# Rebuilding the first part of a fused attention-and-MLP kernel: projections during the layernorm, a software-pipelined MLP and gate, operands of the first head pair staged ahead

## The chip, the cores and the metric

The kernel runs on one core of one Trainium2 chip. The metric is device time in microseconds (us): the median over the executions of one kernel, beside the kernel before on the same chip. Executions are sorted into a fast and a slow state; for this one-core kernel, slow means over 1.5% above the fastest execution of the same kernel. All executions that verdicts use are of the fast state. A profile is one execution of its kernel, with one exception (named below) a fast one; three kernels ran only once, so their state is unknown. Engines are PE (TensorE matmuls), PEld (its weight loads), DVE (VectorE), ACT (ScalarE), POOL (GpSimd) and SP (SyncE); "SPq" and "ACTq" are the queues in which SyncE and ScalarE issue DMAs. PEclk or "clock" is the TensorE clock granted, as a share of full speed.

## The reference

Forward and backward pass of one block, sequence 2048, width 512, 32 heads of 16, MLP width 1792, all in bf16. The kernel returns the output and the gradients of x, wqkv, wo, w1, b1, w2 and b2.

```
xn  = layernorm(x)
qkv = xn @ wqkv                                # attention branch
s   = softmax(q k^T / 4) v @ wo
y   = layernorm(xn)                            # gate branch
g   = silu(gelu(y @ w1 + b1) @ w2 + b2)
out = x + s * g                                # and the vjp of all this for grad_out
```

The first part, which the change rebuilds, makes xn, y, q, k and v, the MLP's hidden layer, the gate, and d = (grad_out * g) @ wo^T. Attention (16 pairs of heads, forward and backward together) follows and takes most of the time; the weight gradients close the kernel. Attention reads its operands from scratch tensors in HBM, which the first part fills.

## The kernel before

Each part of the first stage runs over all 2048 rows (16 tiles of 128) before the next starts. Cuts are marked.

```python
def ln_batch(src_of_t, dst, rstd_all, tagn):
    for t in range(NT):
        nc.vector.bn_stats(...);  nc.vector.bn_aggr(...)
    nc.scalar.activation(out=rstd_all[:], in_=mv[:, :, 1], func=ACT.Sqrt, ...)
    nc.vector.reciprocal(out=rstd_all[:], in_=rstd_all[:])
    for t in range(NT):
        nc.vector.tensor_scalar(out=dst[:, t, :], in0=src_of_t(t), scalar1=mv[:, t, 0:1],
                                scalar2=rstd_all[:, t:t + 1], op0=ALU.subtract, op1=ALU.mult)
ln_batch(..., xn, ...)
for t in range(NT): transpose_to(nc, psT, xnT, xn[:, t, :], ...)    # TensorE transposes
ln_batch(..., y, ...)
for t in range(NT): transpose_to(nc, psT, yT, y[:, t, :], ...)
# ... k and v of 16 tiles, then a maximum of |k|^2 over all rows, then q of 16 tiles (needs it) ...
for sh in range(2):                                   # halves of 1024 rows
    for fc in range(FC):                              # w1: 14 blocks
        h1row = wk.tile([128, S // 2], bf16, name="h1row")     # 3 buffers
        # 2 x (4 matmuls, + b1 on VectorE, gelu on ScalarE), store to H1T_s
    for t8 in range(8):                               # w2, 14 matmuls, then the gate in one chain
        # m_bf = ps + b2; sg = sigmoid(m_bf); gB0 = m_bf * sg; dso = dot * gB0
        # transpose dso; q1 = ((1 - sg) * gB0 + sg); gB1 = q1 * dot; store
        # projection of the tile before
# attention then loads pair 0 from HBM, lays it out in Pad and transposes it by DMA, all 2048 rows
```

Of the kernel before, what the change touches and what calls it, by code (L numbers as in the profile page):

```python
# [16 lines left out]
NT = S // 128  # L17
# [19 lines left out]
def ln_tile(nc, wk, x_t, out_t, rstd_col, eps_t):  # L37
    st = wk.tile([128, nc.vector.BN_STATS_DIM], f32, name="ln_st")
    mv = wk.tile([128, nc.vector.BN_AGGR_DIM], f32, name="ln_mv")
    nc.vector.bn_stats(out=st[:], in_=x_t)  # L40
    nc.vector.bn_aggr(out=mv[:], in_=st[:])
    nc.scalar.activation(out=rstd_col, in_=mv[:, 1:2], func=ACT.Sqrt, bias=eps_t[:], scale=1.0)
    nc.vector.reciprocal(out=rstd_col, in_=rstd_col)
    nmr = wk.tile([128, 1], f32, name="ln_nmr")
    nc.vector.scalar_tensor_tensor(out=nmr[:], in0=mv[:, 0:1], scalar=-1.0, in1=rstd_col, op0=ALU.mult, op1=ALU.mult)
    nc.scalar.activation(out=out_t, in_=x_t, func=ACT.Identity, bias=nmr[:], scale=rstd_col)


def transpose_to(nc, psp, dst3, src_nat, ident, nblk, t, eng_toggle):
    pt = psp.tile([128, nblk, 128], bf16, name="tp_ps", tag="tp")  # L50
    for b in range(nblk):
        nc.tensor.transpose(pt[:, b, :], src_nat[:, b * 128:(b + 1) * 128], ident[:])
    if eng_toggle % 2 == 0:
        nc.vector.tensor_copy(out=dst3[:, :, t * 128:(t + 1) * 128], in_=pt[:])
    else:
        nc.scalar.copy(out=dst3[:, :, t * 128:(t + 1) * 128], in_=pt[:])


def phase_pre(ctx, tc, k, A_x, A_wqkv, A_wo, B_w1, B_b1, B_w2, B_b2, grad_out, dbg):
    nc = tc.nc  # L60
    x2 = A_x.flatten_outer_dims()
    go2 = grad_out.flatten_outer_dims()
    with ExitStack() as c1:
        pA = c1.enter_context(tc.tile_pool(name="preA", bufs=1))
        xnT = pA.tile([128, IC, S], bf16, name="xnT")
        dsoT = pA.tile([128, IC, S], bf16, name="dsoT")
        yT = pA.tile([128, IC, S], bf16, name="yT")
        psT = c1.enter_context(tc.tile_pool(name="pre_psT", bufs=2, space=PSUM))
        psA = c1.enter_context(tc.tile_pool(name="pre_psA", bufs=5, space=PSUM))
        wts = c1.enter_context(tc.tile_pool(name="pre_w", bufs=1))  # L70
        wqkv_sb = wts.tile([128, IC, 3 * D], bf16, name="wqkv_sb")
        w1_sb = wts.tile([128, IC, F], bf16, name="w1_sb")
        w2_sb = wts.tile([128, FC, D], bf16, name="w2_sb")
        wo_sb = wts.tile([128, IC, D], bf16, name="wo_sb")
        mlp_big = c1.enter_context(tc.tile_pool(name="mlp_big", bufs=1))
        mlp_wk = c1.enter_context(tc.tile_pool(name="mlp_wk", bufs=3))

        with ExitStack() as c0:
            big0 = c0.enter_context(tc.tile_pool(name="pre_ln", bufs=1))
            wk0 = c0.enter_context(tc.tile_pool(name="pre_lnwk", bufs=4))  # L80
            xin = c0.enter_context(tc.tile_pool(name="pre_xin", bufs=4))
            xv = x2.rearrange("(t p) d -> p t d", p=128)
            xq = []
            for q4 in range(4):
                xt4 = xin.tile([128, 4, D], bf16, name="xt4")
                (nc.sync if q4 % 2 == 0 else nc.scalar).dma_start(out=xt4[:], in_=xv[:, q4 * 4:(q4 + 1) * 4, :])
                xq.append(xt4)
                if q4 == 0:
                    nc.scalar.dma_start(out=wqkv_sb[:], in_=A_wqkv.rearrange("(c p) f -> p c f", p=128))
            nc.scalar.dma_start(out=w1_sb[:], in_=B_w1.rearrange("(c p) f -> p c f", p=128))  # L90
            nc.sync.dma_start(out=w2_sb[:], in_=B_w2.rearrange("(c p) d -> p c d", p=128))
            nc.scalar.dma_start(out=wo_sb[:], in_=A_wo.rearrange("(c p) b -> p c b", p=128))
            xn = big0.tile([128, NT, D], bf16, name="xn")
            y = big0.tile([128, NT, D], bf16, name="y")

            def ln_batch(src_of_t, dst, rstd_all, tagn):
                st = big0.tile([128, NT, nc.vector.BN_STATS_DIM], f32, name="ln_st" + tagn)
                mv = big0.tile([128, NT, nc.vector.BN_AGGR_DIM], f32, name="ln_mv" + tagn)
                for t in range(NT):
                    nc.vector.bn_stats(out=st[:, t, :], in_=src_of_t(t))  # L100
                    nc.vector.bn_aggr(out=mv[:, t, :], in_=st[:, t, :])
                nc.scalar.activation(out=rstd_all[:], in_=mv[:, :, 1], func=ACT.Sqrt, bias=k.eps_t[:], scale=1.0)
                nc.vector.reciprocal(out=rstd_all[:], in_=rstd_all[:])
                for t in range(NT):
                    nc.vector.tensor_scalar(out=dst[:, t, :], in0=src_of_t(t), scalar1=mv[:, t, 0:1], scalar2=rstd_all[:, t:t + 1],
                                            op0=ALU.subtract, op1=ALU.mult)
            ln_batch(lambda t: xq[t // 4][:, t % 4, :], xn, k.rstd1, "1")
            for t in range(NT):
                transpose_to(nc, psT, xnT, xn[:, t, :], k.ident_bf, IC, t, 1)
            ln_batch(lambda t: xn[:, t, :], y, k.rstd2, "2")  # L110
            for t in range(NT):
                transpose_to(nc, psT, yT, y[:, t, :], k.ident_bf, IC, t, 1)
            nc.sync.dma_start(out=k.XN_s.rearrange("(t p) d -> p t d", p=128), in_=xn[:])
            nc.scalar.dma_start(out=k.Y_s.rearrange("(t p) d -> p t d", p=128), in_=y[:])

        with ExitStack() as c0:
            big = c0.enter_context(tc.tile_pool(name="p15_big", bufs=1))
            wk = c0.enter_context(tc.tile_pool(name="p15_wk", bufs=3))
            stg = c0.enter_context(tc.tile_pool(name="p15_stg", bufs=1))
            nc.vector.tensor_scalar(out=wqkv_sb[:, :, 0:D], in0=wqkv_sb[:, :, 0:D], scalar1=0.25, scalar2=None, op0=ALU.mult)  # L120
            NS = [stg.tile([128, NPAIR, 4, 2, NATW], bf16, name=f"NS{i}") for i in range(2)]
            for i in range(2):
                nc.gpsimd.memset(NS[i][:, :, :, :, 0:1], 1.0)
            NQ = [stg.tile([128, NPAIR, 4, 2, 17], bf16, name=f"NQ{i}") for i in range(2)]
            kmaxrun = big.tile([128, H], f32, name="kmaxrun")
            nc.vector.memset(kmaxrun[:], 0.0)
            for t in range(NT):
                pk = psA.tile([128, 512], f32, name="pk", tag="mm")
                pv = psA.tile([128, 512], f32, name="pv", tag="mm")
                for ic in range(IC):  # L130
                    nc.tensor.matmul(pk[:], lhsT=xnT[:, ic, t * 128:(t + 1) * 128], rhs=wqkv_sb[:, ic, D:2 * D],
                                     start=(ic == 0), stop=(ic == IC - 1))
                for ic in range(IC):
                    nc.tensor.matmul(pv[:], lhsT=xnT[:, ic, t * 128:(t + 1) * 128], rhs=wqkv_sb[:, ic, 2 * D:3 * D],
                                     start=(ic == 0), stop=(ic == IC - 1))
                ns = NS[(t // 4) % 2]
                kpv = ns[:, :, t % 4, :, :]
                nc.scalar.copy(out=kpv[:, :, :, 1:17], in_=pk[:].rearrange("p (a j c) -> p a j c", a=NPAIR, j=2))
                nc.vector.tensor_copy(out=kpv[:, :, :, 17:33], in_=pv[:].rearrange("p (a j c) -> p a j c", a=NPAIR, j=2))
                if t % 4 == 3:  # L140
                    (nc.sync if (t // 4) % 2 == 0 else nc.scalar).dma_start(
                        out=k.NAT_s[:, :, t - 3:t + 1, :].rearrange("a p t c -> p a t c"), in_=ns[:].rearrange("p a t j c -> p a t (j c)"))
                sq = wk.tile([128, H, DH], f32, name="sqk")
                kk = kpv[:, :, :, 1:17]
                nc.gpsimd.tensor_tensor(out=sq[:].rearrange("p (a j) c -> p a j c", j=2), in0=kk, in1=kk, op=ALU.mult)
                kn2 = wk.tile([128, H], f32, name="kn2")
                nc.vector.reduce_sum(out=kn2[:], in_=sq[:], axis=AX.X)
                nc.vector.tensor_tensor(out=kmaxrun[:], in0=kmaxrun[:], in1=kn2[:], op=ALU.max)
# [25 lines left out]
        with ExitStack() as c0:  # L174
# [29 lines left out]
            for sh in range(2):  # L204
# [15 lines left out]
                for t8 in range(8):  # L220
# [23 lines left out]
                    if t >= 1:  # L244
                        do_proj(t - 1)
# [316 lines left out]
def attention_core(ctx, tc, NAT_s, NATQ_s, Oall, dQall, dKVT_out, ident_f32, H1T_s, GP_s, npairs=16, nqc=4):  # L562
# [365 lines left out]
    for f in load_ops(0):  # L928
        f()
# [158 lines left out]
```

## Time and profile before

| what | before |
|---|---|
| time, median (lowest to highest) | 2443.22 us (2431.95 to 2455.26), 3 runs |
| profiled execution | span 2431.6 us, mean clock 0.947 |
| first attention matmul | 286.9 us |
| from there to the end | 2144.7 us |
| PE busy in the first 287 us | 183.5 us |

The first attention matmul splits the span in two: what lies before it is the stage that was rebuilt, what lies behind it should not move. The prediction shows the lines on which its reading rests. One line more matters for what follows. It is one group of the profile's instructions by line and shape; behind the bar are the busy time and the mean ns of one.

```profile
L239 POOL TENSOR_SCALAR q<-sg 128x512 bf16<-128x512 bf16 x16 | 13.0, 815 | 85.3 <-ACT sg L229 85.3
```

This is GpSimd's multiply and add with two constants on a tile of 128 x 512. Its other two-operation instructions on such tiles (L651, 0.62 us each) are multiply and add as well: the kernel before has no subtract and multiply on GpSimd, so there was no duration to take for one.

### The profile page before, as it was taken

The page shows a single profiled execution, that of the slowest core. Times are in us where ns is not written, and L with a number is a line of the kernel's source. Part 1 is how long each engine was busy: PE and PEld are TensorE (multiplying, and loading weights), DVE is VectorE, ACT ScalarE, POOL GpSimd, SP SyncE. Part 2 cuts the span into 40 slices and gives each one's busy share as a digit, 9 for nine tenths or more (in the row PEclk, how much of TensorE's full clock was granted, in tenths as well). Part 3 has the DMA queues.
Part 4 walks back from the last instruction along what each step waited for, and adds up shares of the span by engine and source line. Part 5 has one row for each costly group of instructions (what it writes and reads, how often), then busy time and mean ns, then how long its engine had stood idle before and what let it go on. Part 6 is the DMA issues. An engine that isn't in the chain of part 4 may idle for free.

```text
span 2431.6 us, 47757 instructions
## 1 busy us (share of the span) xinstructions
PE 2206.3 (91%) x18448; PEld 745.9 (31%) x18448; DVE 1824.6 (75%) x3094; ACT 1811.6 (75%) x2102; POOL 1154.4 (47%) x1870
## 2 busy tenths in 40 slices
PE   3688599999999999999999999999999999789997
PEld 2233122222222222222222222222222223334446
DVE  5666379998899889989998977978998895303641
ACT  3254279999899999999998988979999996010231
POOL 0433444666646475665656554646656465300020
PEclk8899679999899999999999988969999999999999
DMA  5355499999999999999999999999999999999466
GB/s 188 110 185 182 113 206 241 248 246 239 230 243 238 241 246 238 250 246 246 239 245 240 232 221 212 248 193 230 244 249 236 247 230 256 263 252 264 139 97 126
DMA packets 1743126, 534.89 MB, mean 220 GB/s; under 512 B 1664433, under 2 KB 1721906, under 8 KB 1742898
## 3 DMA queue, kind: packets, MB, share of 16 engines
q1 hardware_dynamic: 1671554, 449.37, 91.9%
q10 hardware_dynamic: 61104, 54.93, 7.9%
q0 software_dynamic: 10240, 27.54, 3.8%
q8 instruction: 144, 2.36, 0.4%
q14 instruction: 84, 0.69, 0.1%
HBM read 52.83 MB, written 62.66 MB: 47 GB/s over the span
## 4 chain that ended last, share of the span: by engine, by line
PE 37%; ACT 18%; DMA 16%; issue 3%; DVE 2%; POOL 2%; ACTq 0%; SPq 0%; POOLq 0%; DVEq 0%
DMA tg<-eg 11%; ACT eg L745 8%; ACT e L753 8%; PE d L731 7%; PE s L719 6%; PE X L789 6%; PE X L801 3%; PE Z L897 2%; PE ps_dy L491 2%; PE ps_dhg L476 2%; PE X L813 2%; PE ps_dw L437 2%; PE ps_dwq L414 1%; DMA hgc<-DH1T_s 1%; PE ps_dw L550 1%
## 5 line engine op out<-in xcount | busy, mean ns | idle before, releaser
L763 DVE TENSOR_TENSOR eg<-d,eg 128x512 bf16<-128x512 f32 x2048 | 1349.6, 688 | 210.0 <-PE d L731 73.8
L745 ACT ACTIVATE eg<-s 128x1024 bf16<-128x1024 f32 x1024 | 1040.9, 1035 | 80.4 <-PE d L731 50.3
L731 PE MATMUL d<-QDT,KVT 32*128 32x512 bf16 x2048 | 812.5, 397 | 0.1
L753 ACT ACTIVATE e<-t 128x1024 bf16<-128x1024 f32 x640 | 663.4, 1037 | 45.1 <-PE t L705 42.8
L719 PE MATMUL s<-QDT,KVT 32*128 32x512 bf16 x2048 | 412.6, 398 | 64.8 <-ACT eg L745 44.6
L801 PE MATMUL X<-eg,NAT 128*32 128x512 bf16 x2048 | 417.3, 404 | 0.0
L789 PE MATMUL X<-eg,Lc 128*32 128x512 bf16 x2048 | 416.9, 404 | 0.0
L813 PE MATMUL X<-eg,NAT 128*17 128x512 bf16 x2048 | 410.4, 398 | 0.0
L731 PEld LDWEIGHTS <-KVT 32*128 32x128 bf16 x2048 | 186.7, 91 | 349.5 <-issue 349.5
L885 PE MATMUL Z<-e,W 128*32 128x512 bf16 x1280 | 257.6, 398 | 10.9 <-POOL W L852 8.7
L705 PE MATMUL t<-KVT,QDT 32*128 32x512 bf16 x1280 | 256.4, 394 | 6.1 <-ACT eg L745 5.9
L719 PEld LDWEIGHTS <-KVT 32*128 32x128 bf16 x2048 | 118.3, 91 | 320.9 <-issue 318.9
L897 PE MATMUL Z<-tg,W 128*32 128x512 bf16 x2048 | 208.9, 392 | 0.0
L846 POOL TENSOR_TENSOR W<-NATQd,rL 128x128 bf16<-128x128 bf16 x64 | 25.8, 403 | 371.0 <-DVE rL L830 371.0
L789 PEld LDWEIGHTS <-Lc 128*32 128x32 bf16 x2048 | 99.1, 93 | 287.0 <-issue 287.0
L652 POOL TENSOR_TENSOR bg_v<-bg_t 128x512 f32<-128x512 f32 x56 | 57.9, 1034 | 207.1 <-ACT bg_t L667 207.1
L885 PE MATMUL Z<-tg,W 128*32 128x512 bf16 x768 | 155.1, 400 | 0.0
L801 PEld LDWEIGHTS <-NAT 128*32 128x32 bf16 x2048 | 99.3, 94 | 168.9 <-issue 168.9
L911 DVE TENSOR_TENSOR acc<-Z,acc 128x512 f32<-128x512 f32 x192 | 130.7, 681 | 10.8 <-PE Z L897 10.8
L272 POOL TENSOR_TENSOR dx<-lnb_prod,lnb_dy 128x512 bf16<-128x512 f32 x16 | 21.0, 1312 | 236.7 <-DMA dout<-in_grad_out_dram 213.6
L885 PEld LDWEIGHTS <-W 128*32 128x32 bf16 x2048 | 109.1, 93 | 36.4 <-issue 16.8
L813 PEld LDWEIGHTS <-NAT 128*17 128x17 bf16 x2048 | 93.3, 88 | 60.7 <-issue 60.7
(168 smaller groups left out, 2733.8 us busy)
## 6 DMA issues: line engine op xcount, KB each, us to landing
HGT_s<-hgT SPq DMA_DIRECT2D x2, 3584.0 KB
bg_x<-H1T_s POOLq DMA_DIRECT2D x56, 128.0 KB, 5.7
GP_s<-bg_m POOLq DMA_DIRECT2D x56, 128.0 KB, 5.7
gp<-GP_s ACTq DMA_DIRECT2D x8, 896.0 KB, 9.3
DH1T_s<-dh1T SPq DMA_DIRECT2D x4, 1792.0 KB
NAT<-NAT_s POOLq DMA_DIRECT2D x16, 264.0 KB, 6.5
GB_s<-gB ACTq DMA_DIRECT2D x16, 256.0 KB, 2.0
tg<-eg SPq DMA_TRANSPOSE x256, 8.9
```

The costliest lines, as they stand in the source:

```text
L705: nc.tensor.matmul(t[:, hj, :], lhsT=op["QDT"][r:r + 32, q0:q0 + 128], rhs=op["KVT"][r:r + 32, kc * 512:(kc + 1) * 512], start=True, stop= ...
L719: nc.tensor.matmul(s[:, hj, :], lhsT=op["KVT"][r:r + 32, kb * 128:(kb + 1) * 128], rhs=op["QDT"][r:r + 32, qc * 512:(qc + 1) * 512], start ...
L731: nc.tensor.matmul(d[:], lhsT=op["KVT"][r:r + 32, kb * 128:(kb + 1) * 128], rhs=op["QDT"][r:r + 32, qc * 512:(qc + 1) * 512], start=True, ...
L745: nc.scalar.activation(out=cur["eg"][1][:, :, kb % 4, :, :].rearrange("k b h q -> k h b q"), in_=st_s.pop(g)[:].rearrange("k h (b q) -> k ...
L753: nc.scalar.activation(out=e[:], in_=st_t.pop(g)[:], func=ACT.Exp)
L763: nc.vector.tensor_tensor(out=gts[:, kb % 4, hj, :].rearrange("k (b q) -> k b q", b=4), in0=ds[hj][:].rearrange("k (b q) -> k b q", b=4), ...
L789: nc.tensor.matmul(X[64 + 32 * hj:96 + 32 * hj, :], lhsT=Lc[:], rhs=et[:, :, kb % 4, hj, :], start=(kb == 0), stop=False, skip_group_check ...
L801: nc.tensor.matmul(X[32 * hj:32 * hj + 32, :], lhsT=NATt[:, kb, hj, 1:33], rhs=et[:, :, kb % 4, hj, :], start=(kb == 0), stop=(kb == 15), ...
L813: nc.tensor.matmul(X[64 + 32 * hj:64 + 32 * hj + 17, :], lhsT=NATt[:, kb, hj, 0:17], rhs=gts[:, kb % 4, hj, :], start=False, stop=(kb == 1 ...
L885: nc.tensor.matmul(Z[32 * hj:32 * hj + 32, :], lhsT=blk[j]["W1"][:, qb, hj, :], rhs=ev[:, hj], start=(i == 0), stop=False, tile_position=( ...
L897: nc.tensor.matmul(Z[c:c + 32, :], lhsT=blk[j]["W2"][:, qb, hj, :], rhs=gv[:, :, hj, qb, :], start=(i == 1), stop=(i >= 2), tile_position= ...
L911: nc.vector.tensor_tensor(out=av, in0=Z[:], in1=av, op=ALU.add)
```

## The change

The intent is to let TensorE begin with the projections after 512 rows of the layernorm instead of 2048, and then never stop until attention. In outline:

```diff
-            ln_batch(lambda t: xq[t // 4][:, t % 4, :], xn, k.rstd1, "1")
+            def ln1(g):                                   # 512 rows
+                mv, rs = stats(g, src, k.rstd1, "1")
+                norm(nc.vector if g == 0 else nc.gpsimd, xn[g], src, mv, rs)   # (x - mean) * rstd
+                if g == 0:
+                    ...                                   # TensorE transposes
+                else:
+                    nc.sync.dma_start_transpose(out=xnT[...], in_=xn[g]...)
+            def ln2(g):
+                nc.sync.dma_start(out=k.XN_s[...], in_=xn[g][:])
+                ...
+                nc.sync.dma_start_transpose(out=yT[...], in_=y[g]...)
+                nc.sync.dma_start(out=k.Y_s[...], in_=y[g][:])
+            ln1(0)
+            ln1(1)
+            hooks = {1: [ln1(2)], 3: [ln1(3)], 5: [ln2(0)], 8: [ln2(1)], 11: [ln2(2)], 14: [ln2(3)]}   # (lambdas)
             for t in range(NT):
+                ...                                       # k, v, q of one tile, evicted by ScalarE
+                for f in hooks.get(t, ()):
+                    f()
+                if t >= 1:
+                    reduce_of(t - 1)
+                if t % 4 == 3:
+                    nc.sync.dma_start(out=k.NAT_s[...], in_=ns...)          # k and v of 512 rows, 2 buffers
+                    nc.sync.dma_start(out=k.NATQq_s[...], in_=NQ...)
+                if t == 3:
+                    nc.scalar.dma_start(out=w2_sb[:], ...)
+                    nc.scalar.dma_start(out=b1_bf[:], ...)                  # element by element
+                    nc.scalar.dma_start(out=b2_bf[:], ...)
...
+            def h1(sc):                                   # w1 for 512 rows
+                    h1row = hp.tile([128, 512], bf16, name="h1row", bufs=6)
+                    ...
+                    nc.sync.dma_start(out=k.H1T_s[...], in_=h1row[:])
+            def m_step(t):                                # one 128-row step of w2
+                dso_tr(t - 2); proj(t - 5); gate(t - 1); slope_out(t - 3, nc.vector); m_mm(t)
+            first = {9: plain, 10: ck, 11: tk, 12: cq(0, 4), 13: tq(0, 4)}   # pair 0, rows of the first block
+            h1(0); h1(1); row_bound()
+            for sc in range(4):
+                for t in range(4 * sc, 4 * sc + 4):
+                    m_step(t)
+                    if t in first: first[t]()
+                if sc + 2 < 4: h1(sc + 2)
```

The bound for the softmax (the maximum of |k|) is applied to q's norms afterwards, so q no longer waits for k. The scale 1/4 moves into q's eviction. The scheduler is off: the written order is the order on each engine. Attention keeps its instructions but for the pair-0 loads and small stores.

## The prediction

> **What bounds the kernel now.** I read the page first: the engines' busy shares and the forty slices, then the busy time by stage, then TensorE's waits in the first stage, then the timeline at the seam to attention.
>
> ```profile
> PE 2206.3 (91%) x18448; PEld 745.9 (31%) x18448; DVE 1824.6 (75%) x3094; ACT 1811.6 (75%) x2102; POOL 1154.4 (47%) x1870
> ...
> PE   3688599999999999999999999999999999789997
> ...
> PEclk8899679999899999999999988969999999999999
> ```
>
> One slice is 60.8 us. TensorE (PE) is nearly full from the sixth slice on; the poor ones are the first five, which is just the part that the change rebuilds. PEclk is low at the start and at the end of this part (8 and 8, then 6 and 7 in slices 5 and 6). The same as numbers (columns: length, then busy us of PE, weight load, VectorE, ScalarE, GpSimd, then clock, DMA share, GB/s):
>
> ```profile
> 0.00:60.00 60.00, 20.26 (x156) 14.23 (x157) 33.77 (x103) 19.13 (x35) 1.08 (x8) 0.87 0.55 186
> 60.00:120.00 60.00, 37.79 (x165) 16.57 (x165) 36.41 (x75) 17.66 (x36) 27.72 (x29) 0.81 0.42 116
> 120.00:180.00 60.00, 50.78 (x242) 22.27 (x241) 43.30 (x79) 31.25 (x53) 20.27 (x21) 0.98 0.54 179
> 180.00:240.00 60.00, 52.11 (x243) 23.02 (x242) 35.88 (x58) 27.20 (x42) 19.22 (x19) 0.94 0.57 190
> 240.00:287.00 47.00, 22.57 (x117) 9.74 (x116) 14.92 (x27) 6.66 (x11) 26.73 (x31) 0.78 0.43 118
> sum 287.00, PE 183.51 PEld 85.82 DVE 164.29 ACT 101.90 POOL 95.02; mean PE 36.70 PEld 17.16 DVE 32.86 ACT 20.38 POOL 19.00
> ```
>
> PE is busy 183.5 of 287 us, no other engine is above 58%, and the DMA engines are half used: nothing is a bound here, the stage is a chain of waits. They are (waiter, awaited, total us, times, longest):
>
> ```profile
> PE tp_ps L52 <- DVE xn L105: 30.9, 2, 30.6
> PE tp_ps L52 <- DVE dso L235: 19.0, 14, 3.8
> PE s L719 <- DMA QDT<-Pad: 17.0, 1, 17.0
> PE pq L155 <- ACT NQ L159: 16.7, 1, 16.7
> PE pv L134 <- ACT NS L138: 7.1, 1, 7.1
> PE tp_ps L52 <- DVE y L105: 6.1, 3, 5.7
> ```
>
> They sum to 96.8 us: the whole first layernorm before any PE work (30.6), the barrier between k/v and q (16.7), the gate chain (19.0), the operand staging of pair 0 (17.0). The seam, in the timeline:
>
> ```profile
> 139.75 10.52 PE L212 MATMUL ps_h<-yT,w_sb 128*128 128x512 bf16 x48
> ...
> 267.98 1.89 PE L190 MATMUL pd<-woT,dsoT 128*128 128x512 bf16 x4 [0.68 <-ACT dsoT L56]
> ...
> 275.10 0.54 POOL L604 DMA_DIRECT2D NATQd<-NATQd_s  x1 [1.11 <-DMA NATQd_s<-ND]
> ...
> 277.14 1.75 SPq L611 DMA_TRANSPOSE KVT<-Pad  x1
> ...
> 282.26 2.47 SPq L619 DMA_TRANSPOSE QDT<-Pad  x1
> ...
> 286.90 0.61 PE L719 MATMUL s<-QDT,KVT 32*128 32x512 bf16 x2 [17.02 <-DMA QDT<-Pad]
> ```
>
> Attention starts at 286.9 us. The first line gives the rate of a dense stream: 48 matmuls of 512 columns in 10.52 us, less the last one's 0.38 us length, over 47 gaps: 0.2157 us each.
>
> **What the Trainium skill says.** (1) "TensorE: Matmul & The Clock Gate", Back-to-back issue gap: about N/2.4 + 2.5 ns warm, 216 ns for 512 columns; the trace's 0.2157 agrees. (2) The same page, Part 1: the array falls to half clock after an idle window of some 3.4 us and returns after about 3.4 us of sustained work. The trace agrees after the idle times (granted 0.50 from 46 to 68 us; from 268 us on). It does not agree on the return: attention ran at 0.50 from 287 to about 331 us with PE busy all the time, and four dips later in attention last 13 to 44 us.[...] (3) "ScalarE: Activation LUTs", What ACT_TABLE_LOAD costs: about 1283 ns per load; the trace's loads average 1283 ns. (4) "DMA: Bandwidth & Descriptors", Specifications: about 358 GB/s to HBM per core; the trace reaches 401 GB/s over 10 to 20 us and 385 in other short pieces, but 52 to 230 in most, so there is room.
>
> **The change, part by part.** PE work that stays: 192 qkv + 224 w1 + 224 w2 + 64 projection = 704 matmuls x 0.2157 = 151.9 us. Of the before's 208 transposes (64 each of xn, y, dso, 16 of wo) 80 stay; the timeline has four in 0.40 us, so 80 x 0.1 = 8 us. The other 128 (13 us) go to eight DMA transposes. Without a wait PE would need 160 us.
>
> I lay the new fixed order out by hand from the before's durations.
> - Lead-in. x comes first on its queue (7.5 us before; I take 6.5). Four statistics at about 0.82 us (0.66 + 0.17), square root and reciprocal 0.8, four normalisations at 0.33: xn of 512 rows at 12 us, first qkv at 12.5 instead of 32 (and there alone; the dense qkv began at 66).
> - qkv. PE 12 x 0.2157 = 2.59 us per 128 rows, 41.4 for 16. ScalarE evicts all three, 3 x 0.6 = 1.8 us, below PE. The array is cold for about 5 us: +2.5. PE is done at 56.4. The DMA-transposed xnT of rows 512 on (GpSimd normalises 4 x 0.82, the transpose 3.9 as in the KVT line) is there at about 23.5, needed at 25.
> - VectorE here is longer than PE. From 15 us: two more statistics batches of 3.3 and four batches of the second layernorm at 5.4 (3.3 + 0.8 + 1.3), 32 norm reductions at 0.68 = 21.8, three small ones 1.1: 6.6 + 21.6 + 21.8 + 1.1 = 51.1, and about 2.3 of waiting for GpSimd: done at 68.4. The first w1 eviction stands behind it, so PE fills six PSUM tiles (5.2 us, to 61.6) and stalls until 69.2: 7.6 us, enough to fall to half clock, +1.7.
> - w1 for the first 1024 rows: 22 remaining tiles x 0.863 = 19, to 91.6. VectorE needs 0.745 per tile and the gelu 0.63, both below PE.
> - w2, gate, projection: per 128 rows PE 14 x 0.2157 + 0.40 + 0.863 = 4.28 us. VectorE 0.68 + 0.42 + 0.71 + 0.42 = 2.2, ScalarE 0.63 + 0.58 + 0.6 = 1.8, GpSimd 0.85 + 1.20 + 1.15 = 3.2: all hidden, since the gate of one tile now runs beside the w2 of the next ones. Before, such a step took 5.25 us (projection to projection, 257.73 to 262.98). 16 x 4.28 = 68.5, plus the last two w1 blocks 24.2, plus 1.5 for the first gate behind two table loads and 1 at the tail.
> - Seam. Operands of pair 0 (rows of the first query block only) are made during steps 9 to 13, so the 17.0 us vanish.
>
> Sum: 12.5 + 41.4 + 2.5 + 5.2 + 7.6 + 1.7 + 19 + 1.5 + 68.5 + 24.2 + 1 = 185.1. For waits that I don't see I add 5: attention starts at about 190, 97 us earlier.
> - Start of attention. The first block has ten matmuls a step. Cold, 16 steps took 37 us (287 to 324); warm, VectorE's two multiplies at 0.69 would set 1.4 us a step, 22 to 24 us. That is up to 15 us more if the array arrives warm and stays so. I give this one chance in three: 5 us.
> - Attention itself and the last part keep their instructions. Added there: 64 more small stores and one more copy per pair on GpSimd, which is half idle. Zero.
>
> 97 + 5 = 102 us: 2443 - 102 = 2341 us.
>
> **The rivals.** (a) VectorE becomes the bound of the qkv stage, worse than I put it. For: 51 us of work against 41 of PE, in one fixed order, with a drain between statistics and their aggregation. Against: PE needs VectorE only from the first w1 eviction. If batches take 20% longer: 10 us lost, 2351. (b) The SyncE queue: nearly all stores and transposes stand in one order, and a transpose that waits for y holds back the k/v store behind it, whose buffer ScalarE wants 1024 rows later. Some 17 MB are asked for in these 44 us, 390 GB/s, above what the trace sustains. For: a 1 MB k/v store takes 6 us to land. Against: much of it slips past 56 us without being missed, and PSUM holds 5 us of slack. Cost 5 to 20 us: 2346 to 2361. (c) Attention starts warm: PE comes from dense 128-row work. Against: a table load and the first exp leave PE idle for about 2 us at the start, and the dips at 650 and 1472 us follow gaps of 1 to 1.5 us. Gain 10 more: 2331. (d) The gain is given back inside attention by clock dips, whose number varies between executions (2432 to 2455 us before). Either way 10 us.
>
> **Range and chances.** All terms are in the stage's own time; (a) and (b) push up, (c) down, (d) both. 2318 to 2372 us. Faster by over 2% needs 49 us of 102: even if half my saving fails it holds: 0.96. Within 2%: 0.035. Slower: 0.005, only if the new buffers' placement hurt attention.
>
> **What would show it.** Right: the first attention matmul at 180 to 200 us; PE waits of the first stage under 30 us in all; one PE gap of some 8 us at the first w1 eviction behind VectorE's reductions; no wait for QDT; the w2 steps about 4.3 us apart. Wrong: PE waiting for ScalarE's k/v copies, these for a store (b); a w1 wait above 15 us (a); clock 1.0 in the first attention block (c); or a steady attention step other than the before's, in which case I have missed an effect of the new buffer placement.

## The result, and the profile after

The changed kernel took 2365.13 us median (2356.44 to 2373.79, 4 runs), the kernel before 2438.12 us (2431.95 to 2455.26, 4 runs); the result is correct. The ratio is 0.969, 95% interval 0.962 to 0.976. Here and below a ratio compares the fast runs of one kernel with those of the other of the same rounds, as the record gives it, so it is not quite the ratio of the medians quoted, which take in slow runs.

| profiled execution | before | after |
|---|---|---|
| span | 2431.6 | 2354.7 |
| mean clock | 0.947 | 0.953 |
| first attention matmul | 286.9 | 210.9 |
| from there to the end | 2144.7 | 2143.8 |

The whole gain, 76 of 77 us, lies ahead of attention. The prediction had the first attention matmul at about 190 us: 21 us are missing. The page of the kernel after, busy tenths in forty slices (now 58.9 us each):

```profile
PE   5799999999999999999999999999999998789997
...
PEclk9898896999999999989999999997999998999999
```

Before, the fifth slice was the last thin one of the stage; now it is the second. Stage by stage, columns as in the prediction (length, busy us of PE, weight load, VectorE, ScalarE, GpSimd, then clock, DMA share, GB/s):

```profile
0.00:60.00 60.00, 35.03 (x141) 15.32 (x144) 34.68 (x82) 21.65 (x42) 46.88 (x42) 0.92 0.70 198
60.00:120.00 60.00, 44.40 (x181) 18.96 (x183) 40.71 (x76) 28.06 (x48) 14.54 (x15) 0.86 1.00 279
120.00:180.00 60.00, 58.88 (x294) 27.23 (x296) 45.01 (x65) 37.07 (x59) 25.99 (x25) 1.00 0.60 202
180.00:211.00 31.00, 30.61 (x164) 14.18 (x168) 21.75 (x29) 13.56 (x26) 29.25 (x33) 1.00 0.68 198
```

From 120 us on PE is full, so the w2 steps run as predicted. The missing time lies in the first two rows. Two things in them were in no term of the prediction's sum: GpSimd is busy 46.9 of the first 60 us, and the DMA share of the second 60 us is 1.00. PE's waits (waiter, awaited, total us, times, longest):

```profile
PE ps_h L190 <- DVE h1row L193: 15.4, 2, 11.5
PE pk L138 <- ACT NSall L143: 12.1, 2, 6.4
PE tp_ps L105 <- DVE xn L93: 10.1, 1, 10.1
PE pk L138 <- DMA xnT<-xn: 2.4, 1, 2.4
```

All waits of PE up to the first attention matmul come to 41 us, where the prediction wanted under 30. The third line is the lead-in, as predicted. The others are w1 waiting for VectorE's eviction, k's projection waiting for ScalarE's eviction, and the third 512 rows' transpose. What did those two engines wait for?

```profile
DVE h1row L193 <- DMA H1T_s<-h1row: 14.4, 1, 14.4
...
ACT NSall L143 <- DMA NAT_s<-NSall: 9.7, 1, 9.7
...
ACT NSall L143 <- DMA w_sb<-in_B_w_dram: 6.6, 1, 6.6
```

VectorE waits for a store of h1row to free a row buffer; ScalarE waits once for a k/v store to free NSall (two buffers of 512 rows), and once in its own queue, where it is still issuing the bias loads behind the load of w2 (the page names this wait after the weights). The timeline around the k/v store (start, length, what; in brackets the idle time before and what ended it):

```profile
39.31 8.28 POOL L93 TENSOR_SCALAR xn<-x_all,ln_mv,rstd 128x512 bf16<-128x512 bf16 x4
...
47.62 1.32 SPq L108 DMA_TRANSPOSE xnT<-xn  x1
49.03 0.67 SPq L156 DMA_DIRECT2D NAT_s<-NSall  x1
...
56.47 0.60 ACT L143 CAST NSall<-pk 128x512 bf16<-128x512 f32 x1 [9.67 <-DMA NAT_s<-NSall]
57.12 1.86 PE L138 MATMUL pk<-wqkv_sb,xnT 128*128 128x512 bf16 x4 [5.77 <-ACT NSall L143]
```

Read it upwards from PE. PE waits for ScalarE, which waits for the store, which SyncE issues at 49.03, just after the last xnT transpose at 47.62. That transpose stands ahead of the store in SyncE's order, and its input is ready only when GpSimd has ended four normalisations at 47.59. The four take 8.28 us, where the prediction had 4 x 0.82. Meanwhile the DMA engines are nearly idle (20 to 30 us: share 0.24, 54 GB/s), and all that should have flowed then flows from 50 us on. The second stop:

```profile
82.85 4.04 DVE L193 TENSOR_SCALAR h1row<-ps_h,b1c 128x512 bf16<-128x512 f32 x6
...
95.54 11.48 SPq L195 DMA_DIRECT2D H1T_s<-h1row  x14
101.32 5.36 DVE L193 TENSOR_SCALAR h1row<-ps_h,b1c 128x512 bf16<-128x512 f32 x8 [14.43 <-DMA H1T_s<-h1row]
102.12 16.84 PE L190 MATMUL ps_h<-yT,w_sb 128*128 128x512 bf16 x64 [11.45 <-DVE h1row L193]
```

VectorE fills the six row buffers by 86.89; their stores are issued only from 95.54, behind the queue's backlog of other stores, and the seventh eviction starts at 101.32.

### The profile page after: what moved, and what is told of

The parts are those of the page before. It is cut to its first block, busy times and chain, and to the rows that moved or that the text cites. A ratio compares the mean times of both kernels' runs of the same rounds, so it can differ in the third digit from the quotient of the medians.

```text
span 2354.7 us, 47532 instructions
## 1 busy us (share of the span) xinstructions
PE 2189.2 (93%) x18285; PEld 733.8 (31%) x18320; DVE 1802.3 (77%) x3002; ACT 1810.8 (77%) x2098; POOL 1218.3 (52%) x1968
## 4 chain that ended last, share of the span: by engine, by line
PE 51%; ACT 22%; DMA 11%; POOL 7%; issue 4%; DVE 4%; SPq 0%; ACTq 0%; POOLq 0%; DVEq 0%
ACT e L789 10%; ACT eg L781 10%; PE d L767 9%; PE s L755 8%; PE X L825 8%; DMA tg<-eg 5%; PE X L837 4%; PE Z L933 3%; PE X L849 2%; PE ps_dhg L548 2%; PE ps_dy L563 2%; PE ps_h L190 2%; PE ps_m L202 2%; PE ps_dw L509 2%; PE ps_dw L622 1%
```

## The experiments

Twelve kernels ran. Theory, in short: the missing 21 us are GpSimd's slow normalisation, which delays SyncE's order and with it everything behind. Rivals: SyncE's order by itself; ScalarE's bias loads; saturated DMA engines; and, for the attention side, the granted clock. The clean measure is the time of the first attention matmul, called T below. Total times scatter by 20 us and more between executions of one kernel, whatever the first stage does. T is read from one profiled execution of each kernel and is good to some 4 us (210.9 to 214.8 in four kernels whose first stage is the same or as good as the same).

### Normalisation on VectorE

```diff
-                norm(nc.vector if g == 0 else nc.gpsimd, xn[g], src, mv, rs)
+                norm(nc.vector, xn[g], src, mv, rs)
```

> The normalisation of rows 512 on moves from GpSimd to VectorE. In the changed kernel it took GpSimd 8.3 us per 512 rows (2.07 us each, 0.82 in the prediction), and behind it stood the transposes and, in SyncE's order, the first k/v store. Theory A (this duration started the chain of waits): ScalarE's wait for the first k/v store falls from 9.7 us to under 3, VectorE's wait for an H1T store from 14.4 us to under 7, and the first attention matmul comes at 192 to 200 us instead of 210.9; time 2345 to 2355. Rival D (the DMA engines are saturated from 50 to 105 us by volume, whenever the stores start): the first attention matmul moves by less than 5 us, to 206 or later.

T came to 198.6 us, 12.3 earlier. The NAT_s wait is gone. ScalarE's wait in its own queue (7.5 us) stays and makes PE wait 6.6; VectorE still waits 12.6 us for H1T_s, where under 7 was expected. Time 2349.08 us (2326.76 to 2371.33, the last a slow run) against 2450.13 before, ratio 0.959 (0.948 to 0.969). So GpSimd's part in it is shown.

### Which of the instruction's features is slow: constants

The same subtraction and multiplication on GpSimd, but with constants in place of the two per-partition columns. This gives a wrong result on purpose.

```diff
+                    for i in range(4):
+                        nc.gpsimd.tensor_scalar(out=xn[g][:, i, :], in0=src[:, i, :], scalar1=0.0, scalar2=1.0,
+                                                op0=ALU.subtract, op1=ALU.mult)
```

> Wrong result on purpose: the same GpSimd normalisations of rows 512 on, but with the two scalars as constants instead of one value per partition. If the per-partition scalars are what makes them slow, one falls from 2.07 us to about 0.8 us, and the first attention matmul comes at 194 to 202 us. If GpSimd is slow for another reason (VectorE beside it, the strides), it stays near 2.07 and nothing moves.

One instruction took 1937 ns, so the columns are not the cause. T was 202.9 us: the constants need no statistics, so GpSimd starts earlier, and the NAT_s wait shrank to 6.4 us. Time 2342.14 us, one run.

### Multiply and add in place of subtract and multiply

The same numbers as x * rstd + (-mean * rstd), still on GpSimd and still with per-partition columns. VectorE makes the second column.

```diff
+                    nc.vector.scalar_tensor_tensor(out=nmr[:], in0=mv[:, :, 0], scalar=-1.0, in1=rs, op0=ALU.mult, op1=ALU.mult)
+                    for i in range(4):
+                        nc.gpsimd.tensor_scalar(out=xn[g][:, i, :], in0=src[:, i, :], scalar1=rs[:, i:i + 1],
+                                                scalar2=nmr[:, i:i + 1], op0=ALU.mult, op1=ALU.add)
```

> GpSimd keeps the normalisation of rows 512 on, as multiply and add (x times rstd, plus minus mean times rstd, one small VectorE instruction more per 512 rows) in place of subtract and multiply. The form that took 0.82 us in the kernel before was multiply and add; the one with constants in place of the per-partition scalars was subtract and multiply and took 1.94. If the pair of operations decides, one takes 0.8 to 1.0 us and the first attention matmul comes at 196 to 201 us. If not, about 2 us and 210 to 211.

The group lines of the three kernels, first the changed kernel, then constants, then multiply and add:

```profile
L93 POOL TENSOR_SCALAR xn<-x_all,ln_mv,rstd 128x512 bf16<-128x512 bf16 x12 | 24.8, 2087 | 9.9 <-DVE rstd L88 9.9
```

```profile
L104 POOL TENSOR_SCALAR xn<-x_all 128x512 bf16<-128x512 bf16 x12 | 23.0, 1937 | 3.8 <-DMA x_all<-in_A_x_dram 3.8
```

```profile
L106 POOL TENSOR_SCALAR xn<-x_all,rstd,nmr 128x512 bf16<-128x512 bf16 x12 | 9.0, 767 | 10.3 <-DVE nmr L104 10.0
```

2087, 1937 and 767 ns on the same tile: the pair of operations decides; the kind of its scalars makes 0.15 us of it. Which of the two operations is the slow one was not tried. The Trainium skill, "GPSIMD Engine Reference", section "Elementwise — side-by-side cycle accounting", states 1.8 cycles per element and 769 ns measured for 512 elements as its best case. Multiply and add meets this with 767 ns here (with constants, later in these kernels, it takes 0.62 us); subtract and multiply takes 2.7 times that. T was 200.5 us, 10.4 earlier, and the result is correct; the NAT_s wait fell to 0.6 us. ScalarE's wait in its own queue (7.3 us) and VectorE's for H1T_s (15.6 us) stay, so this one duration accounts for about half of the missing 21 us. Time 2360.19 us, one run.

### Bias loads out of ScalarE's queue

```diff
-                    nc.scalar.dma_start(out=b1_bf[:], ...)      # at t == 3
-                    nc.scalar.dma_start(out=b2_bf[:], ...)
+            nc.sync.dma_start(out=b1_bf[:], ...)                # after ln1(1)
+            nc.sync.dma_start(out=b2_bf[:], ...)
```

> The two small bias loads leave ScalarE's queue and go to SyncE's, before the second transpose. ScalarE stood in its queue from 31.1 to 38.0 us at these loads, and PE waited 6.4 us for its k copy. Theory E: that PE wait goes, but the next one (for the k/v store, 9.7 us) takes most of it over, so the first attention matmul comes 0 to 4 us earlier, at 207 to 211. If the wait was a loss of its own, it comes 6 us earlier, at 204 to 205.

ScalarE's wait in its own queue vanished, yet T was 211.3 us: no gain. On SyncE's queue the issue of the two loads took 0.57 and 1.10 us, on ScalarE's 0.95 and 5.47 us. So they are not slow to issue by themselves; on ScalarE's queue they stood right behind the 1.8 MB load of w2, and whether that is the reason was not tried. The NAT_s wait was still 9.0 us and PE's wait for ScalarE 10.4. The store that sets the pace is issued at the same time as ever, and a ScalarE that comes earlier only waits longer for it. Time 2382.46 us (2357.39 to 2387.37), ratio 0.973 (0.964 to 0.982).

### k/v stores ahead of the hooks

```diff
+                if t % 4 == 3:
+                    ...                                  # the NAT_s and NATQq_s stores, moved up
                 for f in hooks.get(t, ()):
                     f()
```

> Only the order in SyncE's queue: the k/v and q stores of a group of 512 rows are issued before the hook of that step (the third xnT transpose, and later the third second-layernorm group), not after. GpSimd's 2.07 us stay. Theory B (a store held back behind a transpose that waits): the first store goes out at about 41 us instead of 49.0, ScalarE's wait of 9.7 us falls under 3, and the first attention matmul comes 5 to 10 us earlier, at 201 to 206. If A alone is right, the wait only moves to the transposes: 208 to 211.

SyncE's queue in this kernel:

```profile
39.08 0.53 SPq L152 DMA_DIRECT2D NAT_s<-NSall  x1
...
47.62 1.62 SPq L108 DMA_TRANSPOSE xnT<-xn  x1
```

The store now goes out at 39.08, ten microseconds earlier, past the transpose that still waits for GpSimd until 47.62. ScalarE's NAT_s wait is gone. But T was 206.6 us, only 4.3 earlier, about its scatter: PE still waits 10.0 us in all for ScalarE, and 3.3 for a transposed xnT. Of the 10.0, the bias loads make 4.7. The other 5.3 us are a second way in which GpSimd's slow normalisation reaches PE: it delays GpSimd's squares for the norms, VectorE's reductions wait for these, and the statistics of the second layernorm stand behind them. ScalarE's square root waits 9.0 us for the statistics, and k's copy stands behind it:

```profile
57.54 0.30 ACT L87 ACTIVATE rstd<-ln_mv,eps_t 128x4 f32<-128x4 f32 x1 [8.96 <-DVE ln_mv L85]
...
58.38 1.86 PE L138 MATMUL pk<-wqkv_sb,xnT 128*128 128x512 bf16 x4 [5.30 <-ACT NSall L143]
```

Time 2367.06 us (2358.2 to 2387.74), ratio 0.971 (0.960 to 0.981). The wait for the store was real, but the order in SyncE's queue is not enough by itself.

### All three together

> The normalisation on VectorE, the bias loads on SyncE and the k/v stores first, together. With the normalisation on VectorE alone the first attention matmul came at 198.6 us and PE's largest waits were 13.5 us (a w1 tile, behind VectorE's wait for an H1T store) and 6.6 us (ScalarE in its queue at the bias loads). The second must now go whole, since no store wait is left to take it over: 190 to 194 us, time about 2340. If the bias loads cost nothing even now: 197 to 199.

T was 194.6 us, 16.3 earlier (190 to 194 was expected). PE's wait for ScalarE's copies fell from 12.1 to 2.9 us. T is 4.0 us earlier than with the normalisation on VectorE alone, where PE waited 6.6 us behind the bias loads. The bias move would then be worth something once the wait that hid it is gone; but the store order was changed too, and 4 us is what T scatters, so what each of the two is worth is not shown. What stays is the wait of w1: 12.2 us, behind VectorE's 12.1 for H1T_s. The time, however, was 2363.41 us (2349.19 to 2370.27) against 2438.97, ratio 0.974 (0.965 to 0.982): no better than the changed kernel. In the profiled execution the stretch from T to the end was 2171.7 us instead of 2143.8. This is the clock, see below.

### The H1T stores of the first 512 rows on another queue

```diff
-                    nc.sync.dma_start(out=k.H1T_s[...], in_=h1row[:])
+                    (nc.gpsimd if sc == 0 else nc.sync).dma_start(out=k.H1T_s[...], in_=h1row[:])
```

> As the three together, and the H1T stores of the first 512 rows go out from GpSimd's queue, not from SyncE's. Theory Q (these stores wait in SyncE's order behind the late x-norm, y and k/v stores): VectorE's wait for an H1T store falls from over 10 us to under 3, and the first attention matmul comes 6 to 10 us before that of the three together, at 181 to 187 us. Rival D (the 16 DMA engines are saturated then, whichever queue): the wait stays above 8 us and the start moves by less than 2.

On top of all three. T was 193.5 us, no more than its scatter, with the wait cut into pieces but not shortened:

```profile
DVE h1row L193 <- DMA H1T_s<-h1row: 13.2, 4, 6.3
```

The first of these stores is issued at 73.30 us, where the three together issued it at 78.84; but in both kernels VectorE goes on only about 5.8 us later, and here it then stops three times more. So SyncE's queue is at most a small part of what holds them. In this kernel the DMA share is 1.14, 1.08 and 1.09 in the three 10-us stretches from 50 to 80 us: the 16 engines are full. The Trainium skill, "DMA: Bandwidth & Descriptors", section "Issuing engines are not separate DMA queues", says just that: DMAs started by different engines end on the same 16 DMA engines and interleave. This run agrees. One rival is left: GpSimd's stores have a median of 5.6 us from issue to landing in this kernel, SyncE's H1T stores 1.8, so GpSimd's queue may be the slower one; in the backlog itself both took about 5.8 us. Time 2350.42 us (2346.33 to 2369.04), ratio 0.971 (0.960 to 0.982).

### More row buffers

```diff
-                    h1row = hp.tile([128, 512], bf16, name="h1row", bufs=6)
+                    h1row = hp.tile([128, 512], bf16, name="h1row", bufs=14)
```

> As the three together, with 14 h1row buffers in place of 6. With H1T stores in another queue VectorE still waited 13.2 us for them, so the 16 DMA engines have a backlog there, not the queue. Theory D2 (the backlog costs time only because VectorE runs out of row buffers): the wait falls under 3 us and the first attention matmul comes at 184 to 188 us instead of 194.6. If the backlog comes out at another buffer, PE keeps 8 us or more of waits after the first w1 tiles and the start is 191 or later.

Also on top of all three. The waits of the two engines:

```profile
PE ps_h L190 <- DVE h1row L193: 6.5, 2, 3.9
...
DVE h1row L193 <- DMA H1T_s<-h1row: 6.1, 1, 6.1
```

The wait was expected under 3 us. The DMA engines are as full as before (share 1.18, 1.15 and 1.12 from 50 to 80 us), but VectorE runs further ahead. T was 186.9 us, 24.0 earlier than the changed kernel and 7.7 earlier than the three alone. Time 2359.18 us (2333.21 to 2377.3, the last a slow run) against 2453.26, ratio 0.955 (0.945 to 0.965); the plain means of the fast runs give 0.961.

### Filling PE's gap at the start of attention

Rival (c) of the prediction was a warm start of attention. In the changed kernel it did not happen: the first block (first score matmul to the first of the next kind, t) took 37.2 us, as before (37.1). Ten dummy matmuls of 128 rows were put into the 2 us in which PE waits for the first exponential.

```diff
         emit_d(g, 1)
+        if g == 0:
+            zf = ps_z.tile([128, 512], f32, name="zf", tag="z")
+            for _ in range(10):
+                nc.tensor.matmul(zf[:], lhsT=OP[0]["KVT"][:, 0:128], rhs=OP[0]["QDT"][:, 0:512], start=True, stop=True)
         emit_t(g)
```

> The changed kernel with ten extra 128-row matmuls into an unused PSUM bank at the first attention step, where PE idles about 2 us for the table load and the first exp. They take about 2.2 us and nothing reads them. If that gap is what drops the clock, it stays 1.0 and the first block, 37.2 us from the first s to the first t matmul in the changed kernel, takes 22 to 26 us, the time 10 to 15 us less. If attention's own light work drops it, the clock is 0.50 a few us later and the block takes 34 to 38 us.

The windows of the changed kernel, then of this one:

```profile
220.00:230.00 10.00, 10.00 (x50) 1.96 (x46) 6.62 (x10) 4.72 (x5) 6.76 (x10) 0.50 1.03 183
...
240.00:250.00 10.00, 10.00 (x53) 2.05 (x52) 6.31 (x10) 5.38 (x7) 2.94 (x5) 0.50 0.98 224
```

```profile
220.00:230.00 10.00, 10.00 (x80) 2.95 (x76) 9.71 (x16) 7.01 (x9) 6.65 (x10) 1.00 0.97 188
...
240.00:250.00 10.00, 9.69 (x58) 2.33 (x54) 5.85 (x10) 6.94 (x9) 6.11 (x15) 0.50 1.26 246
```

With the gap filled, the clock stayed at full speed, PE did 80 matmuls in ten microseconds instead of 50, and the first block took 27.6 us. So the drop at the start comes from the gap of 2 us, and attention's small matmuls can run warm. But at 231 us PE idled for 0.52 us, waiting for ScalarE, and soon after for 0.34 us, and at about 233 us the clock fell to 0.50 until about 260 us. Why so little idle time was enough there is not shown. The dip was put off and shortened (27 us instead of 41), not avoided, and nothing of the 10 us is left at the end: from T on, this profile has 2143.3 us, the changed kernel's 2143.8. T was 211.1 us, time 2357.72 us (2344.4 to 2359.3), ratio 0.971 (0.963 to 0.979): no gain over the changed kernel that these runs resolve, where 10 to 15 us were expected.

### One dummy matmul in each step

```diff
+        if g < 16:                                       # in place of ten at g == 0
+            zf = ps_z.tile([128, 512], f32, name="zf", tag="z")
+            nc.tensor.matmul(zf[:], ...)
```

> The changed kernel with one extra 128-row matmul per step in the sixteen steps of the first attention block, nothing in the 2 us gap before it. With the gap filled, the clock had stayed 1.0 to 232 us and the block took 27.6 us. Theory L (attention's 32-row matmuls count as too little work to bring the clock back, 128-row work would): it returns to 1.0 within 10 us of the drop and the block takes 26 to 31 us. If once down it stays down whatever runs, each step is 0.43 us longer at half clock: 40 to 45 us.

This failed. The gap of 2 us was open again, the clock was at 0.50 from about 220 to 300 us, and one full-size matmul a step did not bring it back; it only cost time. The first block took 45.2 us; time 2383.82 us, one run. Whether a denser filling would raise the clock is not known.

### The versions that put everything together

The three edits, 14 row buffers and the filled gap; once with the normalisation on VectorE, once on GpSimd as multiply and add.

> All that helped in one kernel (normalisation of every group on VectorE, bias loads on the SyncE queue, k/v stores ahead of the hooks, 14 row buffers for H1T) and the ten dummy matmuls in the gap at the start of attention. Theory (terms of the first stage add up; the clock gap costs some 10 us of the first block): first attention matmul at 186 to 188 us as in the kernel with 14 row buffers, no wait of ScalarE for NAT_s, first block 27 to 30 us at clock 1.0 at first, time 2320 to 2350 us and ratio 0.950 to 0.965. Rival (the clock in attention decides whatever the first stage does: what is not lost at the start is lost in a later dip): first matmul at the same place, but time within 5 us of the changed kernel, ratio 0.968 or more.

> As the run before, with the normalisation of groups 1 to 3 on GpSimd as multiply plus add instead of on VectorE, so VectorE is free of 12 x 0.33 us in the qkv stage. If VectorE is what bounds the qkv stage once the other waits are gone, the first w1 eviction and so the first attention matmul come 2 to 4 us earlier (183 to 186 us); if the saturated DMA engines set it, nothing moves (186 to 188). Time within 5 us of the run before either way, since the clock's scatter is larger.

The first: T 185.5 us, 2351.76 us (2320.94 to 2361.67, 6 runs, three of them of the slow state, the profiled one too) against 2460.15, ratio of the fast runs 0.955 (0.947 to 0.963). The second: T 190.3 us, so later and not earlier, with more wait of w1 (9.7 against 6.1 us); 2337.87 us (2319.32 to 2352.89), ratio 0.958 (0.951 to 0.965). Both are correct. Neither of the two expectations (183 to 186, or 186 to 188) was met by the second. Relieving VectorE of twelve instructions buys nothing that these runs show. Both kernels beat the changed one, by 18 us at equal clock (the table below); what the filled gap adds to the 14 row buffers (2.5 us there) is within the errors. The clock stayed up at the start of attention in both and fell some 20 us later, as in the run that only filled the gap.

### Why the times follow T so poorly: the granted clock

Within each kernel, executions differ mainly by their mean clock. Over all fast executions of the kernels with three or more of them (61 executions), a straight line through each kernel's executions with one common slope gives 17.4 us per 0.01 of mean clock, and leaves 3.8 us (standard deviation) unexplained. The record's own verdict against the kernel before is "faster" for the changed kernel, for the normalisation on VectorE, for the 14 row buffers and for everything with the normalisation on VectorE, and "unclear" for the others that ran more than once; so totals alone do not rank these kernels. With each fast execution moved to a clock of 0.95 by this slope, an estimate worked out from the runs' times and clocks, the kernels stand as follows; the standard errors are about 2 us.

| kernel | T | mean of fast runs | the same at clock 0.95 |
|---|---|---|---|
| kernel before | 286.9 | 2440.3 | 2428.1 |
| changed kernel | 210.9 | 2365.1 | 2363.4 |
| changed kernel, gap filled | 211.1 | 2354.8 | 2357.0 |
| bias loads moved | 211.3 | 2377.4 | 2360.5 |
| stores first | 206.6 | 2370.0 | 2359.2 |
| normalisation on VectorE | 198.6 | 2341.6 | 2353.2 |
| all three | 194.6 | 2361.6 | 2348.1 |
| all three, other queue | 193.5 | 2354.1 | 2349.3 |
| all three, 14 row buffers | 186.9 | 2350.5 | 2347.6 |
| everything, norm on VectorE | 185.5 | 2332.4 | 2345.1 |
| everything, multiply and add | 190.3 | 2338.5 | 2345.4 |

At equal clock all three are 15.3 us ahead of the changed kernel, with T 16.3 earlier. The 14 row buffers then take another 7.7 us off T and only 0.5 off this total, and the changed kernel is only 64.7 us ahead of the one before, with T 76.0 earlier. Part of that is the adjustment itself: a first stage without long waits also keeps its clock, and that clock is inside the mean that is evened out. By the profiles the first stage ran at a mean clock of 0.88 before, 0.94 in the changed kernel, 0.96 with all three and 0.98 with 14 row buffers. Giving this part back with the same slope, an estimate worked out from these clocks, puts the changed kernel 79 us ahead of the one before, and all three 20 and the 14 row buffers 23 us ahead of the changed kernel, where T says 76, 16 and 24. Within these errors the total follows T all the way, and no loss in attention is shown. By the same token, a kernel that fills the gap changes the clock itself, so its place in this table does not show what the filling is worth.

## Why the prediction was right or wrong

The time predicted was 2341 us in a range of 2318 to 2372; measured were 2365.13, inside the range, and the verdict (faster by over 2%) was held at 0.96. The predicted saving was 102 us, the measured one 73 us against the runs of the same rounds and 76 in T. Of the 24 us between 2341 and 2365, about 21 are the late T and 5 the warm start that did not come; the range was wide enough to hold both.

- **What bounded the kernel** (a chain of waits in the first 287 us, nothing after): right. 76 of the 77 us between the profiles lie there.
- **Lead-in 12.5 us**: right; the first transposes ran at 10.07 us, the first projection at 12.21.
- **PE done with qkv at 56.4**: wrong, 74.1 by the start of w1. This is the step that failed. The term was "GpSimd normalises 4 x 0.82": its 0.82 came from a multiply and add, and a subtract and multiply takes 2.09 us. The run with multiply and add shows that this one number was worth 10 us of T; PE's wait behind the bias loads (6.4 us) was in no term either.
- **VectorE done at 68.4, so the first w1 eviction then**: 82.85, 14.4 late because qkv was late; the stall itself was 3.9 us, shorter than the 7.6 predicted.
- **Rival (b), the SyncE order**: it came, in the very form described ("holds back the k/v store behind it, whose buffer ScalarE wants 1024 rows later"), but behind a transpose of xn and not of y, and fed by the slow normalisation. The prediction left it out of the sum with at most the 5 us for unseen waits. Its argument that 17 MB in 44 us, 390 GB/s, are "above what the trace sustains" fits too: the DMA engines were idle early and full from 50 to 100 us, with 268 to 312 GB/s, and the H1T stores then cost 11.45 us of PE at w1. This second stop was in no term.
- **The account**: 185.1 (the bare sum) + 14.4 (stall at w1 ends at 83.6 instead of 69.2) + 11.45 (H1T) = 210.95; measured 210.9. So the rest of the sum held as a total; its 5 us for unseen waits are not in it. One slip stands inside the prediction: "to 91.6" is 89.9 by its own terms (the cold 1.7 us counted twice), and the final sum has it right.
- **w2 steps of 4.28 us**: right; from 172.61 to 201.95 us seven steps take 4.19 us each (4.11 to 4.39, projection to projection), and PE is 58.9 of 60 us busy from 120 to 180.
- **The seam's 17 us vanish**: right, no wait for QDT is left, only the 2 us for the first exponential.
- **"a wait of w1 above 15 us (a)"** was the sign for VectorE as the bound. The waits sum to 15.4 us, but the long one is a buffer waiting for its store, so the sign alone would have misled: read what the awaited engine itself waits for.
- **Warm start, one chance in three, 5 us**: it did not come. The clock fell to 0.50 through the 2-us gap, as the argument against it said, and the run that filled the gap shows that this is the cause: with it filled, attention's 32-row matmuls ran at clock 1.00 for some 20 us.
- **Attention itself unchanged**: right, 2143.8 against 2144.7 us.

So the mechanism and the stage were right. About half of what is missing comes from one duration, taken from an instruction that only looked alike; the rest from waits that the sum left out, on the bias loads and above all on row buffers behind full DMA engines.

## What to carry to other kernels

Take a duration only from the same engine with the same pair of operations: GpSimd's multiply and add and its subtract and multiply differ by 2.7, and one rewrites into the other for one small instruction. In one in-order DMA queue, put a store whose buffer somebody wants ahead of a transfer whose input is not ready; when the DMA engines themselves are full, more buffers help and another queue may not (here 7.7 and 1.1 us). Where a clock varies from run to run, judge a local edit by the time at which the next stage starts, and compare totals at equal clock only where the edit leaves the clock alone.

## What the Trainium skill lacked or had wrong

- "GPSIMD Engine Reference", "Elementwise — side-by-side cycle accounting": it gives 769 ns for 512 elements as the best case, and has nothing that tells one pair of operations from another. Runs: 128 x 512 bf16, multiply and add 767 ns with columns, 618 ns with constants (L687 of the changed kernel), subtract and multiply 2087 ns with columns and 1937 ns with constants.
- "TensorE: Matmul & The Clock Gate", Part 1: its table has the clock fall after an idle window of about 3.4 us and return after about 3.4 us of sustained work; a later paragraph of that part lets shorter idles drop it in one kernel, but gives no length. Runs: a gap of 2.0 us was enough to lose it, in the kernel with the filled gap it fell after idle times of only 0.52 and 0.34 us, and with PE busy nearly all the time it stayed at 0.50 for 41 us in the changed kernel and 27 us in the kernel with the filled gap; one full-size matmul in each step did not bring it back.
- "DMA: Bandwidth & Descriptors": the section cited says that the time to initiate a DMA is usually small beside the DMA itself. The issue of the small load of b2, behind the loads of w2 and b1, held ScalarE's queue for 5.47 us of the 9.4 us until it landed, and its next copy for 6.62 us; on SyncE's queue the same issue took 1.10 us. What makes the difference was not tried.
